# Mixture-of-experts tiles: tokens turned by VectorE in 32x32 blocks instead of by TensorE

## Chip, cores, metric

The kernel runs on 1 core of one Trainium2 chip. The metric is the device time of one execution in microseconds (us). Before the change it is 1062.39 us, the median of 3 runs (1062.15 to 1063.95).

## What is computed

The reference is an attention layer whose output feeds a mixture of experts. The attention has 8 batches, 8 heads, 576 positions and head size 64, and a bias that a small network makes of relative positions. Its output, 4608 tokens of 512 numbers, goes to 8 experts, one expert per token:

```
logits = x @ w_gate + modality_bias[modality_id]
e_idx = argmax(logits)
...
h = maximum(x[mask] @ w1[e], 0.0)
out[mask] = gate_w[mask, None] * (h @ w2[e])
```

`w1[e]` is 512 x 1024 and `w2[e]` 1024 x 512, all in float32.

## The kernel before

The attention part and the routing take the first 600 us or so. Routing (`route_steps`) writes each token's row, its 512 numbers, its gate and its index, into a table `xg` in device memory (516 columns), sorted by expert. The rest of the time goes to the experts.

**Tiles.** Each expert's rows are worked in tiles of 256 tokens (`tile`, L1201). The first five tiles (t = 0 to 4, `moe_first`, L1264) use experts that have a full tile before the last batch is routed; what is left of the routing runs beside tiles 0 to 3 as hooks (`beside`). The others run in `moe_rest` (L1282); a few very small remainders (`tiny_steps`, L1332) are put between the steps of three of them. The tables with the order of the tiles are computed on the chip.

**One tile.** Every float32 operand is split in a high part, rounded to TensorE's fp32r format, and a low part, the rest; a product is three products of parts. For a tile:

- `phase1` (L1152): four steps `f2`, each with two groups of 12 matmuls of 256 columns. A group takes the 4 products (w1 high, x high), then the 4 of (w1 high, x low), then the 4 of (w1 low, x high). ScalarE then writes `hh`, the high part of relu (L1168), and VectorE `hl`, its low part (L1169).
- `phase2` (L1174): two halves, w = 0 and 1, of 128 tokens; each has 24 matmuls of 512 columns, first 16 that alternate `hh` and `hl` over the 8 chunks of w2 high, then 8 with w2 low. ScalarE scales the result by the gate into `mo` (L1191) and GpSimd writes it to the output rows with an indirect DMA (L1192).
- Beside phase 1, the second layer's weights are split in four parts (`wsplit(1, ...)`, L1128 on ScalarE, L1129 on VectorE); after it the first layer's weights for the next tile, in four parts (`wsplit(0, ...)`).
- After half w = 0 of phase 2, `middle` (L1229) calls `xprep(t + 1, w)` (L1139) for both halves of the next tile.

**xprep before.** `load_rows` (L1081) brings the tile's 256 rows as one DMA, 128 partitions by two neighbouring tokens of 516 columns, into `gx`. `xprep` turns one half: four TensorE transposes of 128x128 into a PSUM bank (L1146), a ScalarE copy from there to `xh` (L1149), and a VectorE subtraction that reads PSUM and `xh` and writes `xl` (L1150). GpSimd copies the gate and the index (L1143, L1144).

**First tile.** The preparation of tile 0 is a hook at the end of the attention: `xprep(0, 0)` and `xprep(0, 1)` in steps 0 and 1 after the last pair of heads (`first_tiles`, L1241).

**Queues.** All engines run their instructions in the order in which the program issues them (a manual schedule). SyncE issues the loads: `load_new(t + 2, 0)` after phase 2, the rows of tile t + 2 at the start of tile t (from t = 4 on), and w2 after phase 1. The weight loads carry a condition and move nothing when the expert stays the same. The first layer's weights come as one DMA of 2 MB into 128 partitions (L1076).

Of the kernel before, what the change touches and what calls it, by code (L numbers as in the profile page):

```python
# [11 lines left out]
F32 = mybir.dt.float32  # L12
# [4 lines left out]
ALU = mybir.AluOpType  # L17
# [4 lines left out]
P = 128  # L22
# [8 lines left out]
DM = H * D  # L31
F = 1024
NDC = DM // P
NFC = F // P
TS = 256
NS = 32
NT = 3
XW = DM + 4
# [24 lines left out]
def n_tiles(n_tok):  # L63


    return -(-(n_tok - E * NS) // TS), (n_tok + E * (TS - 1)) // TS
# [42 lines left out]
class Attn:  # L109
# [766 lines left out]
    def moe_early(self, cp):  # L876

        nc = self.nc
        lo, hi = n_tiles(self.n_tok)
        self.n_kt = self.n_tab // TS - 1  # L880
        self.T = hi
        self.sure = lo
        n_tt = max(E, hi + 1 - self.K)
        one = cp.tile([1, 2 * E + self.n_kt + n_tt], F32, name="one")
        nc.sync.dma_start(one, self.io["c_one"])
        self.eb, self.iota = one[:, 0:E], one[:, E : 2 * E]
        self.kt, self.tt = one[:, 2 * E : 2 * E + self.n_kt], one[:, 2 * E + self.n_kt :]
        self.gates = cp.tile([P, 4], F32, name="gates")
        self.gk = cp.tile([1, E, self.n_kt], F32, name="gk")
        self.ge = cp.tile([1, n_tt, E], F32, name="ge")  # L890
        self.tf = cp.tile([1, 4, n_tt], F32, name="tabf")
        self.ev = {nm: cp.tile([1, E], F32, name=nm) for nm in ("cnt", "off", "cum", "val", "taken", "start", "big", "lim")}
        self.pad = [cp.tile([1, 4 + E], F32, name=f"pad{k}") for k in range(3)]
        for t in self.pad:
            nc.vector.memset(t, 0.0)
        self.ev["nt"] = self.pad[0][:, 4:]
        self.ex = cp.tile([1, 1], F32, name="last_expert")
        nc.vector.memset(self.ex, -1.0)
        nc.vector.memset(self.ev["taken"], 0.0)
        self.tabs = {nm: cp.tile([1, 4, n], I32, name=f"tab_{nm}") for nm, n in (("first", max(1, self.K)), ("big", hi + 1 - self.K), ("tiny", E))}  # L900
        self.idt = cp.tile([P, 4], I32, name="idt")
        self.gl = cp.tile([1, n_tt, E], F32, name="gl")
        self.tl = cp.tile([1, n_tt], F32, name="tl")
        self.ids_q = [cp.tile([P, 1], I32, name=f"idsq{k}") for k in range(NT)]
        self.quad = cp.tile([P, 1], F32, name="quad")
        nc.sync.dma_start(self.quad, self.io["c_quad"])

        slots = self.NBm.rearrange("p (c q h) k -> p c q (h k)", c=4, q=NP)
        w = [slots[:, :, q, 0 : 2 * DM] for q in range(NP)]
        rest = [slots[:, :, q, 2 * DM : 2 * S] for q in range(NP)]  # L910
        self.wst, self.ws = [w[0], w[1]], [w[2], w[3]]
        self.xr = [slots[:, c, 2, XW * j : XW * j + XW] for c, j in ((0, 0), (1, 0), (3, 0), (0, 1), (1, 1))]
        self.lt = slots[:, 2, 2, 0:XW]
        self.hq = [rest[0], rest[3]]
        self.gx = [self.NBr[:, k : k + 2, 0:XW] for k in (0, 2)]
        d = self.n_pair % 2
        qt = [self.QK[k].rearrange("p a w -> p (a w)") for k in (d, 1 - d)]
        self.xh = [t[:, 0 : NDC * TS].rearrange("p (c w) -> p c w", c=NDC) for t in qt]
        self.xl = [t[:, NDC * TS : 2 * NDC * TS].rearrange("p (c w) -> p c w", c=NDC) for t in qt]

    def moe_tiles(self, st):
        tc = self.tc
        mp = st.enter_context(tc.tile_pool(name="mp", bufs=1))
        self.whi = [mp.tile([P, NDC, F], F32R, name="w1hi"), mp.tile([P, NFC, DM], F32R, name="w2hi")]
        self.wlo = [mp.tile([P, NDC, F], F32R, name="w1lo"), mp.tile([P, NFC, DM], F32R, name="w2lo")]
        self.hh = mp.tile([P, NFC, TS], F32R, name="hh")
        self.hl = mp.tile([P, NFC, TS], F32R, name="hl")
        self.mo = [mp.tile([P, DM], F32, name=f"mo{k}") for k in range(2)]
        pp = st.enter_context(tc.tile_pool(name="mps", bufs=1, space=PSUM))
        self.p1 = [pp.tile([P, 2, TS], F32, name=f"p1{k}") for k in range(3)]  # L930
        self.p2 = [pp.tile([P, DM], F32, name=f"p2{k}") for k in range(3)]
        self.at = {}
# [135 lines left out]
        return ("first", t) if t < self.K else ("big", t - self.K)  # L1068

    def load_w(self, nm, t, k, dst, cond=None):  # L1070
        e = self.reg(nm, t, 0, [mybir.EngineType.SP], E - 1)
        c = None if cond is None else self.reg(nm, t, cond, [mybir.EngineType.SP], 1)
        kw = {} if c is None else dict(cond=c)
        src = self.io[("moe_w1", "moe_w2")[k]][ds(e, 1), :, :].rearrange("o (c p) f -> p (o c) f", p=P)
        if k == 0:
            self.nc.sync.dma_start(dst, src, **kw)  # L1076
        else:
            for j in range(2):
                self.nc.sync.dma_start(dst[:, :, DM * j : DM * j + DM], src[:, j::2, :], **kw)

    def load_rows(self, t):  # L1081

        nm, k = self.place(t)
        off = self.reg(nm, k, 1, [mybir.EngineType.SP], E * self.n_tab - TS)
        self.nc.sync.dma_start(self.gx[t % 2], self.xg[ds(off, TS), :].rearrange("(p w) c -> p w c", w=2))

    def rows(self, t):
        return [self.gx[t % 2][:, w, :] for w in range(2)]

    def ids_of(self, t):  # L1090
        return [self.idt[:, (2 * t + w) % 4 : (2 * t + w) % 4 + 1] for w in range(2)]
# [44 lines left out]
        self.nc.scalar.copy(h, w)  # L1136
        self.nc.vector.tensor_tensor(l, w, h.bitcast(F32), op=ALU.subtract)

    def xprep(self, t, w):  # L1139
        nc = self.nc  # L1140
        ps = self.xbank().rearrange("p (c w) -> p c w", c=NDC)
        x = self.rows(t)[w]
        nc.gpsimd.tensor_copy(self.gate(t)[w], x[:, DM : DM + 1])  # L1143
        nc.gpsimd.tensor_copy(self.ids_of(t)[w], x[:, DM + 1 : DM + 2])  # L1144
        for c in range(NDC):
            nc.tensor.transpose(ps[:, c, :], x[:, P * c : P * c + P], self.idf)  # L1146
        sl = slice(P * w, P * w + P)
        xh, xl = self.xh[t % 2], self.xl[t % 2]
        nc.scalar.copy(xh[:, :, sl], ps)  # L1149
        nc.vector.tensor_tensor(xl[:, :, sl], ps, xh[:, :, sl].bitcast(F32), op=ALU.subtract)  # L1150

    def phase1(self, t, before, beside):  # L1152
        nc = self.nc
# [47 lines left out]
    def tile(self, t, beside=None, between=()):  # L1201

        parts = iter(range(NDC))
        beside = beside or (lambda: None)

        def split():
            self.wsplit(1, next(parts))
            beside()

        between = iter(between)  # L1210

        def ahead(f2):
            for f in itertools.islice(between, 1):
                f()
            if t:
                return
            for part in {0: (1,) if self.K else (0, 1), 1: (2,), 2: (3,)}.get(f2, ()):
                self.wsplit_cols(part)
            if f2 == 2:
                self.load_new(1, 0)  # L1220

        if t + 2 > self.K:
            self.moe_rows(t + 2)
        self.phase1(t, ahead, split)
        self.load_new(t + 1, 1)
        for c in range(NDC):
            self.wsplit(0, c)

        def middle(w):  # L1229
            if w == 0 and t + 1 < self.T:  # L1230
                for j in range(2):
                    self.xprep(t + 1, j)
            beside()

        self.phase2(t, middle)
        if t + 2 <= self.K:
            self.moe_rows(t + 2)
        if t + 2 <= self.T:
            self.load_new(t + 2, 0)

    def first_tiles(self):  # L1241

        nc = self.nc
        n = self.n_pair - NP
        at = {}

        def add(pair, u, f):
            at.setdefault((n + pair, u), []).append(f)

        for k, f in enumerate(self.first_table()):  # L1250
            add(*divmod(4 + k, 5), f)
        add(2, 3, lambda: self.load_w("first", 0, 0, self.wst[0]))
        add(2, 2, lambda: self.load_rows(0))
        add(3, 0, lambda: self.load_w("first", 0, 1, self.wst[1]))
        for w in range(2):
            add(4, w, lambda w=w: self.xprep(0, w))
        add(4, 3, lambda: self.wsplit_cols(0))
        return at

# [22 lines left out]
    def moe_rest(self, st):  # L1282
        tc, nc = self.tc, self.nc
# [6 lines left out]
        if K == 0:  # L1290
            self.moe_load(0)
            self.load_new(0, 1)
            for w in range(2):
                self.xprep(0, w)
            self.moe_load(1)
        first = self.sure - 2 * NT
        for t in range(K, self.sure):
            k, odd = divmod(t - first, 2)
# [146 lines left out]
```

## Time and profile before

| | |
|---|---|
| median of 3 runs | 1062.39 us |
| the profiled execution | 1062.4 us |
| its span, first to last instruction | 1060.5 us |
| granted TensorE clock, mean | 0.998 |
| TensorE matmul, busy | 1011.3 us (95%) |
| VectorE, busy | 742.7 us (70%) |
| ScalarE, busy | 666.9 us (63%) |
| GpSimd, busy | 304.4 us (29%) |
| SyncE DMA queue (q1), share of 16 DMA engines | 30.5% |

The page names engines PE (TensorE matmul), PEld (its weight loads), DVE (VectorE), ACT (ScalarE), POOL (GpSimd) and SP (SyncE). "L1146" is line 1146 of the kernel before. Busy time of matmuls overlaps, because they are pipelined: the distance from one start to the next is the time that one takes from the stream. An idle time in brackets stands ahead of a row's instruction, with the engine whose work ended it.

### The profile page before, as it was taken

The page shows a single profiled execution, that of the slowest core. Times are in us where ns is not written, and L with a number is a line of the kernel's source. Part 1 is how long each engine was busy: PE and PEld are TensorE (multiplying, and loading weights), DVE is VectorE, ACT ScalarE, POOL GpSimd, SP SyncE. Part 2 cuts the span into 40 slices and gives each one's busy share as a digit, 9 for nine tenths or more (in the row PEclk, how much of TensorE's full clock was granted, in tenths as well). Part 3 has the DMA queues.
Part 4 walks back from the last instruction along what each step waited for, and adds up shares of the span by engine and source line. Part 5 has one row for each costly group of instructions (what it writes and reads, how often), then busy time and mean ns, then how long its engine had stood idle before and what let it go on. Part 6 is the DMA issues. An engine that isn't in the chain of part 4 may idle for free. (4 is left out here: it accounts for less than half of the span.)

```text
span 1060.5 us, 22805 instructions
## 1 busy us (share of the span) xinstructions
PE 1011.3 (95%) x8388; PEld 801.6 (76%) x8388; DVE 742.7 (70%) x1566; ACT 666.9 (63%) x1284; POOL 304.4 (29%) x489
## 2 busy tenths in 40 slices
PE   6879999999999989999999999999999999999997
PEld 2357776767677767677676789999999999888896
DVE  7886678787787787877879676785556655554544
ACT  6777776777777767677676664455555545454544
POOL 1612333526335253352443411530010111111011
PEclk9999999999999999999999999999999999999999
DMA  6977723234242333343234410122113821152410
GB/s 151 191 158 141 190 54 71 62 66 102 47 78 69 69 76 69 58 93 65 58 74 131 137 41 30 61 86 70 41 41 133 297 67 46 65 184 73 166 42 24
DMA packets 225465, 97.52 MB, mean 92 GB/s; under 512 B 201262, under 2 KB 201646, under 8 KB 225346
## 3 DMA queue, kind: packets, MB, share of 16 engines
q1 hardware_dynamic: 219330, 76.96, 30.5%
q0 software_dynamic: 5920, 19.03, 5.0%
q8 instruction: 68, 1.11, 0.4%
q14 instruction: 51, 0.42, 0.1%
q10 hardware_dynamic: 96, 0.00, 0.0%
HBM read 134.94 MB, written 23.90 MB: 150 GB/s over the span
## 5 line engine op out<-in xcount | busy, mean ns | idle before, releaser
L431 ACT ACTIVATE Eb<-Eb,mn 128x576 f32<-128x576 f32 x288 | 221.7, 771 | 66.4 <-DVE mn L416 66.3
L416 DVE CUSTOM_DVE_ANT_0 Eb<-sps,NBm 128x576 f32<-128x576 f32 x256 | 183.6, 754 | 62.7 <-PE sps L402 53.8
L402 PE MATMUL sps<-QK 64*128 64x288 f32 (+1 forms) x1728 | 171.2, 309 | 2.3 <-DVE mn L416 2.0
L402 PEld LDWEIGHTS sps<-QK 64*128 64x128 f32 (+1 forms) x1728 | 133.8, 185 | 46.1 <-DVE mn L416 15.6
L1166 PE MATMUL p<-QK,w1hi 128*128 128x256 f32 x1136 | 160.9, 284 | 0.0
L446 PE MATMUL eps<-idf,Eb 128*128 128x128 f32 x1024 | 147.7, 279 | 10.6 <-DVE eT L333 8.2
L1169 DVE SCALAR_TENSOR_TENSOR hl<-p,hh 128x512 fp32r<-128x512 f32 x72 | 49.7, 691 | 148.5 <-ACT hh L1168 148.4
L1166 PEld LDWEIGHTS p<-QK,w1hi 128*128 128x128 f32 x1136 | 147.0, 192 | 2.9 <-issue 1.8
L500 PE MATMUL xps<-eT,vraw 128*64 128x288 f32 x1024 | 147.1, 412 | 0.0
L446 PEld LDWEIGHTS eps<-idf,Eb 128*128 128x128 f32 x1024 | 111.3, 140 | 41.4 <-issue 17.7
L1192 POOL DMA_INDIRECT out<-mo,idt x36 | 40.1, 1113 | 317.1 <-ACT QK L1149 234.1
L1168 ACT ACTIVATE hh<-p 128x512 fp32r<-128x512 f32 x72 | 43.1, 599 | 119.9 <-PE p L1166 113.8
L331 ACT ACTIVATE eT<-eps 128x512 f32<-128x512 f32 x160 | 95.0, 593 | 34.1 <-PE eps L446 25.5
L1183 PE MATMUL p<-w2hi,hh 128*128 128x512 f32 x288 | 114.2, 396 | 0.0
L1183 PE MATMUL p<-w2hi,hl 128*128 128x512 f32 x288 | 112.5, 391 | 0.0
L436 POOL COPY rem<-Eb 128x128 f32<-128x128 f32 x128 | 37.5, 294 | 248.2 <-ACT Eb L431 245.2
L500 PEld LDWEIGHTS xps<-eT,vraw 128*64 128x64 f32 x1024 | 65.3, 137 | 53.5 <-issue 19.6
L1129 DVE TENSOR_TENSOR w2lo<-NBm,w2hi 128x1024 fp32r<-128x1024 f32 x72 | 88.2, 1225 | 16.2 <-ACT w2hi L1128 16.2
L333 DVE COPY eT<-eps 128x512 f32<-128x512 f32 x128 | 87.1, 681 | 11.8 <-PE eps L446 11.5
L1166 PE MATMUL p<-QK,w1lo 128*128 128x256 f32 x568 | 91.3, 283 | 0.0
L1129 DVE TENSOR_TENSOR w1lo<-NBm,w1hi 128x1024 fp32r<-128x1024 f32 x72 | 83.2, 1220 | 0.0
L1191 ACT ACTIVATE mo<-p,gates 128x512 f32<-128x512 f32 x36 | 24.8, 690 | 89.4 <-PE p L1183 75.2
(211 smaller groups left out, 1646.2 us busy)
## 6 DMA issues: line engine op xcount, KB each, us to landing
NBm<-moe_w SPq DMA_DIRECT2D x23, 2048.0 KB
NBm<-moe_w SPq DMA_DIRECT2D x44, 1024.0 KB
NBr<-xg SPq DMA_DIRECT2D x20, 516.0 KB
kraw<-k SPq DMA_DIRECT2D x128, 72.0 KB
NBm<-xTb SPq DMA_DIRECT2D x32, 288.0 KB
vraw<-v SPq DMA_DIRECT2D x64, 128.0 KB
xg<-blank SPq DMA_DIRECT2D x9, 516.0 KB
qraw<-q SPq DMA_DIRECT2D x64, 72.0 KB
```

Source lines behind the costliest of these rows:

```text
L331: self.nc.scalar.activation(out, ps, AF.Copy, scale=scale)
L333: self.nc.vector.tensor_copy(out, ps)
L402: nc.tensor.matmul(self.sps[h][:, half, 0:HS], QK[o, q, qs], QK[o, k, HS * half : HS * half + HS], start=i == 0, stop=i == 2, skip_group_c ...
L416: nc.vector.tensor_tensor_reduce(out=e.rearrange("p (t w) -> p t w", t=2), in0=self.sps[h][:, :, 0:HS], in1=nb.rearrange("p (t w) -> p t w ...
L431: self.nc.scalar.activation(e, e, AF.Exp, bias=mn, scale=-1.0, accum_out=sm)
L446: nc.tensor.transpose(ps[:, k, :], e[:, part, P * k : P * k + P], self.idf)
L500: nc.tensor.matmul(ps[o, :], v[:, h, k, :], self.eT[:, h, k, sl], start=half == 1 and k == 0, stop=half == 0 and k == 3, tile_position=(0, ...
L1129: self.nc.vector.tensor_tensor(l, w, h.bitcast(F32), op=ALU.subtract)
L1166: nc.tensor.matmul(ps[:, a, :], w[:, c, fs], x[:, c, :], start=i == 0, stop=i == len(ops) - 1)
L1168: nc.scalar.activation(hh[:, sl, :], ps, AF.Relu)
L1169: nc.vector.scalar_tensor_tensor(hl[:, sl, :], ps, 0.0, hh[:, sl, :].bitcast(F32), op0=ALU.max, op1=ALU.subtract)
L1183: nc.tensor.matmul(ps, h[:, f, sl], m[:, f, :], start=i == 0, stop=i == len(ops) - 1)
```

## The change

The tile's tokens are turned on VectorE. `load_rows` issues five DMAs: for each of four column blocks of 128, the 256 rows of that block land in 32 partitions, token 32a + r in partition r of the block, its 128 numbers at place a; a fifth DMA brings gate and index. One VectorE transpose of 128x1024 in 32x32 blocks (new L1163) then gives a tile `xt` with the hidden dimension on partitions, in the order 32 rows of each 128 per chunk. The rows of w1 are loaded in the same order, by four DMAs into 32 partitions each. The eight TensorE transposes go, and so does the PSUM bank that they used; the ScalarE copy and the VectorE subtraction become one instruction each, of 128x1024, with both inputs in SBUF. The load for the tiny remainders and all of w2 stay as they were.

```diff
     def load_w(self, nm, t, k, dst, cond=None):
...
+        if k == 0 and nm != "tiny":
+            for g in range(NDC):
+                rows = src[:, P * g : P * g + P, :].rearrange("o (c p) f -> p (o c) f", p=32)
+                self.nc.sync.dma_start(dst[32 * g : 32 * g + 32, :, :], rows, **kw)
+            return
...
     def load_rows(self, t):
...
-        self.nc.sync.dma_start(self.gx[t % 2], self.xg[ds(off, TS), :].rearrange("(p w) c -> p w c", w=2))
+        gx, rows = self.gx[t % 2], self.xg[ds(off, TS), :]
+        for g in range(NDC):
+            self.nc.sync.dma_start(
+                gx[32 * g : 32 * g + 32, 0 : NDC * TS].rearrange("r (a x) -> r a x", x=P),
+                rows[:, P * g : P * g + P].rearrange("(a r) x -> r a x", r=32),
+            )
+        self.nc.sync.dma_start(
+            gx[:, NDC * TS : NDC * TS + 4].rearrange("p (w x) -> p w x", w=2),
+            rows[:, DM : DM + 2].rearrange("(w p) x -> p w x", p=P),
+        )
...
-    def xprep(self, t, w):
-        nc = self.nc
-        ps = self.xbank().rearrange("p (c w) -> p c w", c=NDC)
-        x = self.rows(t)[w]
...
-        for c in range(NDC):
-            nc.tensor.transpose(ps[:, c, :], x[:, P * c : P * c + P], self.idf)
-        sl = slice(P * w, P * w + P)
+    def xprep(self, t, x):
...
         xh, xl = self.xh[t % 2], self.xl[t % 2]
-        nc.scalar.copy(xh[:, :, sl], ps)
-        nc.vector.tensor_tensor(xl[:, :, sl], ps, xh[:, :, sl].bitcast(F32), op=ALU.subtract)
+        x = x.rearrange("p (c w) -> p c w", c=NDC)
+        nc.vector.transpose(x, gx[:, 0 : NDC * TS].rearrange("p (a c i) -> p c a i", c=NDC, i=32))
+        nc.scalar.copy(xh, x)
+        nc.vector.tensor_tensor(xl, x, xh.bitcast(F32), op=ALU.subtract)
...
             if w == 0 and t + 1 < self.T:
-                for j in range(2):
-                    self.xprep(t + 1, j)
+                self.xprep(t + 1, self.xt)
...
-        for w in range(2):
-            add(4, w, lambda w=w: self.xprep(0, w))
+        add(4, 0, lambda: self.xprep(0, self.Eb[:, next(self.e_next)].rearrange("p h s -> p (h s)")[:, 0 : NDC * TS]))
```

Where instructions move, in the order of one engine. First TensorE in the middle of phase 2 of an ordinary tile (`p_...` is a PSUM tile of the result, `xps` the bank of the transposes, `NBr` the memory of `gx`), before and then after:

```order
L1183 MATMUL p_7581<-w2hi,hl 128x512
L1183 MATMUL p_7581<-w2lo,hh 128x512 x8
L1146 MATMUL xps_77<-idf,NBr 128x128 x4
L1146 MATMUL xps_78<-idf,NBr 128x128 x4
L1183 MATMUL p_7582<-w2hi,hh 128x512
```

```order
L1198 MATMUL p_7580<-w2hi,hl 128x512
L1198 MATMUL p_7580<-w2lo,hh 128x512 x8
L1198 MATMUL p_7581<-w2hi,hh 128x512
L1198 MATMUL p_7581<-w2hi,hl 128x512
L1198 MATMUL p_7581<-w2hi,hh 128x512
```

Half w = 1 now follows half w = 0 with nothing between them.

Then VectorE at the same place (`QK` is the memory of `xh` and `xl`), before and after:

```order
L1129 TENSOR_TENSOR w2lo<-NBm,w2hi 128x1024
L1129 TENSOR_TENSOR w1lo<-NBm,w1hi 128x1024 x4
L1150 TENSOR_TENSOR QK_73<-xps_77,QK_73 128x4x128
L1150 TENSOR_TENSOR QK_73<-xps_78,QK_73 128x4x128
L1169 SCALAR_TENSOR_TENSOR hl<-p_7579,hh 128x512
```

```order
L1143 TENSOR_TENSOR w2lo<-NBm,w2hi 128x1024
L1143 TENSOR_TENSOR w1lo<-NBm,w1hi 128x1024 x4
L1163 STREAM_TRANSPOSE xt<-NBr 128x1024
L1165 TENSOR_TENSOR QK_73<-xt,QK_73 128x1024
L1184 SCALAR_TENSOR_TENSOR hl<-p_7578,hh 128x512
```

The two subtractions are now a transpose and one subtraction, and between those two ScalarE's copy must run.

Last ScalarE at the end of the attention, where tile 0 is prepared (`eT` and `rT` are the turned attention weights), before and after:

```order
L331 ACTIVATE eT<-eps_717 128x4x128
L1149 CAST QK_72<-xps_78 128x4x128
L331 ACTIVATE eT<-eps_716 128x4x128
L331 ACTIVATE rT<-xps_77 128x512
L1149 CAST QK_72<-xps_78 128x4x128
L331 ACTIVATE xTb_95<-xps_77 128x288
```

```order
L331 ACTIVATE eT<-eps_717 128x4x128
L1164 CAST QK_72<-Eb 128x1024
L331 ACTIVATE eT<-eps_716 128x4x128
L331 ACTIVATE rT<-xps_78 128x512
L331 ACTIVATE xTb_95<-xps_77 128x288
```

The whole copy of tile 0 now stands ahead of the `eT` and `rT` copies, where only its first half stood.

## Rows read from the trace of the kernel before

**Rows 1.** The page, part 1: busy us, share and instructions of each engine.
```profile
PE 1011.3 (95%) x8388; PEld 801.6 (76%) x8388; DVE 742.7 (70%) x1566; ACT 666.9 (63%) x1284; POOL 304.4 (29%) x489
```

**Rows 2.** Waits of PE, 640 to 1060 us: total us, times, longest; the whole answer.
```profile
PE p L1365 <- DVE ht L1358: 0.6, 3, 0.2
```

**Rows 3.** Timeline of PE, an ordinary tile: start us, us, engine, line, what.
```profile
827.87 1.12 PE L1166 MATMUL p<-QK,w1hi 128*128 128x256 f32 x8
828.83 0.64 PE L1166 MATMUL p<-QK,w1lo 128*128 128x256 f32 x4
...
839.38 0.40 PE L1183 MATMUL p<-w2hi,hh 128*128 128x512 f32 x1
...
844.86 1.04 PE L1146 MATMUL xps<-idf,NBr 128*128 128x128 f32 x8
...
851.22 1.11 PE L1166 MATMUL p<-QK,w1hi 128*128 128x256 f32 x8
```

**Rows 4.** Groups of instructions by line: count, busy us, mean ns, idle before.
```profile
L1146 PE MATMUL xps<-idf,NBr 128*128 128x128 f32 x152 | 19.9, 273 | 0.2 <-DVE QK L1150 0.2
L378 DVE STREAM_TRANSPOSE qT<-qraw 128x640 f32<-128x640 f32 x32 | 26.8, 836 | 0.0
L378 DVE STREAM_TRANSPOSE kT<-kraw 128x576 f32<-128x576 f32 x32 | 24.8, 774 | 0.0
L1128 ACT CAST w1hi<-NBm 128x1024 fp32r<-128x1024 f32 x72 | 70.4, 1055 | 0.0
L1129 DVE TENSOR_TENSOR w1lo<-NBm,w1hi 128x1024 fp32r<-128x1024 f32 x72 | 83.2, 1220 | 0.0
```

**Rows 5.** Timeline of DVE, ACT and POOL in the same tile.
```profile
842.30 4.62 DVE L1129 TENSOR_TENSOR w1lo<-NBm,w1hi 128x1024 fp32r<-128x1024 f32 x4
845.78 1.06 ACT L1149 CAST QK<-xps 128x512 fp32r<-128x512 f32 x2
846.66 1.12 POOL L1192 DMA_INDIRECT out<-mo,idt  x1 [16.00 <-ACT QK L1149]
846.84 1.28 DVE L1150 TENSOR_TENSOR QK<-xps,QK 128x512 fp32r<-128x512 f32 x2
```

**Rows 6.** Timeline of tile 0: phase 2 begins, and the subtractions for tile 1.
```profile
627.00 0.47 PE L1183 MATMUL p<-w2hi,hh 128*128 128x512 f32 x1
635.36 1.29 DVE L1150 TENSOR_TENSOR QK<-xps,QK 128x512 fp32r<-128x512 f32 x2
```

**Rows 7.** Timeline from the end of tile 2 to the end of tile 3.
```profile
683.68 1.27 DVE L1150 TENSOR_TENSOR QK<-xps,QK 128x512 fp32r<-128x512 f32 x2
688.00 2.01 DVE L956 TENSOR_TENSOR pad<-pad 1x8 f32<-1x8 f32 x2
688.93 1.05 POOL L845 TENSOR_TENSOR NBm<-NBm,rec 64x512 f32<-64x512 f32 x1
699.40 0.40 PE L1183 MATMUL p<-w2hi,hh 128*128 128x512 f32 x1
700.59 0.67 DVE L1169 SCALAR_TENSOR_TENSOR hl<-p,hh 128x512 fp32r<-128x512 f32 x1
707.86 1.27 DVE L1150 TENSOR_TENSOR QK<-xps,QK 128x512 fp32r<-128x512 f32 x2
```

**Rows 8.** Timeline at the end of the attention, where tile 0 is prepared.
```profile
605.87 0.69 DVE L1150 TENSOR_TENSOR QK<-xps,QK 128x512 fp32r<-128x512 f32 x1 [0.63 <-ACT QK L1149]
606.21 0.62 ACT L331 ACTIVATE rT<-xps 128x512 f32<-128x512 f32 x1
607.64 0.71 PE L491 MATMUL xps<-rT,vrem 128*64 128x288 f32 x4
```

**Rows 9.** SP's timeline (two rows), and one window: us, five engines, PEclk, DMA, GB/s.
```profile
800.29 0.39 SPq L1076 DMA_DIRECT2D NBm<-moe_w  x1
848.36 0.56 SPq L1085 DMA_DIRECT2D NBr<-xg  x1
```
```profile
812.00:814.00 2.00, 2.00 (x19) 2.00 (x18) 1.23 (x1) 0.65 (x3) 0.00 (x0) 1.00 0.00 0
```

More of the change, by code (lines that the diff above doesn't have):

```diff
@@ L914, in moe_early @@
         self.hq = [rest[0], rest[3]]
-        self.gx = [self.NBr[:, k : k + 2, 0:XW] for k in (0, 2)]
+        self.gx = [self.NBr[:, k : k + 2, :].rearrange("p a s -> p (a s)") for k in (0, 2)]
         d = self.n_pair % 2
@@ L927, in moe_tiles @@
         self.hl = mp.tile([P, NFC, TS], F32R, name="hl")
+        self.xt = mp.tile([P, NDC * TS], F32, name="xt")
         self.mo = [mp.tile([P, DM], F32, name=f"mo{k}") for k in range(2)]
@@ L1073, in load_w @@
         kw = {} if c is None else dict(cond=c)
-        src = self.io[("moe_w1", "moe_w2")[k]][ds(e, 1), :, :].rearrange("o (c p) f -> p (o c) f", p=P)
+        src = self.io[("moe_w1", "moe_w2")[k]][ds(e, 1), :, :]
+        if k == 0 and nm != "tiny":
[3 more added lines that the diff above has]
+            return
+        src = src.rearrange("o (c p) f -> p (o c) f", p=P)
         if k == 0:
@@ L1084, in load_rows @@
         off = self.reg(nm, k, 1, [mybir.EngineType.SP], E * self.n_tab - TS)
-        self.nc.sync.dma_start(self.gx[t % 2], self.xg[ds(off, TS), :].rearrange("(p w) c -> p w c", w=2))
-    def rows(self, t):
-        return [self.gx[t % 2][:, w, :] for w in range(2)]
+        gx, rows = self.gx[t % 2], self.xg[ds(off, TS), :]
[8 more added lines that the diff above has]
+        )
     def ids_of(self, t):
@@ L1137, in wsplit_cols @@
         self.nc.vector.tensor_tensor(l, w, h.bitcast(F32), op=ALU.subtract)
-    def xprep(self, t, w):
+    def xprep(self, t, x):
         nc = self.nc
-        ps = self.xbank().rearrange("p (c w) -> p c w", c=NDC)
-        x = self.rows(t)[w]
-        nc.gpsimd.tensor_copy(self.gate(t)[w], x[:, DM : DM + 1])
-        nc.gpsimd.tensor_copy(self.ids_of(t)[w], x[:, DM + 1 : DM + 2])
-        for c in range(NDC):
-            nc.tensor.transpose(ps[:, c, :], x[:, P * c : P * c + P], self.idf)
-        sl = slice(P * w, P * w + P)
+        gx = self.gx[t % 2]
+        for w in range(2):
+            at = NDC * TS + 2 * w
+            nc.gpsimd.tensor_copy(self.gate(t)[w], gx[:, at : at + 1])
+            nc.gpsimd.tensor_copy(self.ids_of(t)[w], gx[:, at + 1 : at + 2])
         xh, xl = self.xh[t % 2], self.xl[t % 2]
-        nc.scalar.copy(xh[:, :, sl], ps)
-        nc.vector.tensor_tensor(xl[:, :, sl], ps, xh[:, :, sl].bitcast(F32), op=ALU.subtract)
+        x = x.rearrange("p (c w) -> p c w", c=NDC)
+        nc.vector.transpose(x, gx[:, 0 : NDC * TS].rearrange("p (a c i) -> p c a i", c=NDC, i=32))
+        nc.scalar.copy(xh, x)
+        nc.vector.tensor_tensor(xl, x, xh.bitcast(F32), op=ALU.subtract)
     def phase1(self, t, before, beside):
@@ L1292, in moe_rest @@
             self.load_new(0, 1)
-            for w in range(2):
-                self.xprep(0, w)
+            self.xprep(0, self.xt)
             self.moe_load(1)
```

## The prediction

> **What bounds the kernel now.** I read the page's busy shares first, then TensorE's waits, then the timeline of one tile, then the rows of the engines that would take over the work. PE is busy 95% of the span [rows 1]; that alone does not say that it is the bound, since matmuls overlap. The list of its waits does: from 640 to 1060 us PE waited 0.6 us in all [rows 2]. In the expert tiles every instruction taken from PE's stream therefore shortens the time, until another engine is late. VectorE has room on the average (70%), but what counts is whether it is ready at the hand-over from one tile to the next.
>
> One ordinary tile lasts 851.22 - 827.87 = 23.35 us [rows 3]. Half w = 0 of phase 2 takes 844.86 - 839.38 = 5.48 us, and the transposes plus half w = 1 take 851.22 - 844.86 = 6.36 us. The eight transposes so cost 0.88 us of the stream, not the 8 x 273 ns that their busy time [rows 4] suggests. Matmuls of phase 1 follow each other at (828.83 - 827.87) / 8 = 0.12 us, those of phase 2 at 5.48 / 24 = 0.228 us.
>
> **What the change removes.** 152 transposes [rows 4] are 19 preparations of eight: one at the end of the attention, 18 in tiles. In tiles: 18 x 0.88 = **15.8 us** off PE's path. The sums below go against the profiled execution, 1062.4 us (span 1060.5), which is the median of the runs within 0.1 us.
>
> **What it adds, on the new chain.** Per tile VectorE turns 128x1024. Rows of the same operation give 774 ns for 576 columns and 836 for 640 [rows 4], 0.97 ns a column; 384 more make 836 + 372 = 1208 ns, and up to 1236 at 1.04 ns, taken as 1.22 us. But those rows read each partition straight through, and the new one hops between runs of 32 numbers; no row shows that. The lower bound is 1.2 us, the upper one twice, 2.4 us; I take 1.22, since the nearest row is the same operation with the same blocks. Then ScalarE's copy of 128x1024, 1.055 us, and VectorE's subtraction, 1.22 us, both from rows of equal shape [rows 4]. The chain is 1.22 + 1.05 + 1.22 = 3.5 us and serial: VectorE waits for ScalarE in the middle. Before, ScalarE's copies (845.78) ran beside VectorE's weight splits (842.30 to 846.92), and the subtractions took 1.28 us [rows 5].
>
> *Ordinary tile.* VectorE is free for it at 846.84 [rows 5], so `xl` would be ready at 850.34. PE would reach the next tile at 851.22 - 0.88 = 850.34; its first four matmuls need only `xh` (ready at 849.1), the fifth needs `xl`, at 850.34 + 4 x 0.12 = 850.82. Margin: 0.48 us, less the hand-offs between engines. It was some 3.6 us. I forecast no stall in the 13 ordinary hand-overs (after tiles 4 to 16), but the cover is thin.
>
> *Tile 0.* The chain starts at 635.36 and ends at 638.86. PE needs `xl` at 627.00 + 2 x 5.48 + 0.48 = 638.44 [rows 6]: **+0.4 us**. Tiles 1 and 2 I take as covered, like the ordinary ones.
>
> *Tile 3.* Here VectorE works off the table of the remaining tiles without a pause. The chain of tile 2 starts at 683.68 and takes 3.5 us where 1.27 were, so what follows starts 2.2 us later. Part of it comes back: the two small subtractions and additions of L956 took 2.01 us because GpSimd was at L845 until 689.98 [rows 7], and that wait now falls on a queue that is behind anyway; I estimate a lag of 0.8 us (between 0 and 2). Then the last `hl` ends at 700.59 + 0.67 + 0.8 = 702.06, while PE, 0.88 earlier, wants it 13 matmuls into phase 2, at 698.52 + 13 x 0.228 = 701.48: 0.6 us. `xl` ends at 707.86 + 0.8 + 3.5 = 712.16, wanted at 698.52 + 0.6 + 10.96 + 0.48 = 710.56: 1.6 us. Together **+2.2 us** (1.4 without a lag, 3.4 with 2 us).
>
> *End of the attention.* VectorE is free at 605.87 - 0.63 = 605.24 [rows 8]. The transpose ends at 606.46, ScalarE's whole copy at 607.51, and only then come `eT` and `rT` of 0.6 us each, done at 608.7. The matmuls of L491 wait for `rT` and started at 607.64: **+1.0 us**. PE's own eight transposes less give nothing there, as it waits. Bounds: -0.8 (PE's saving counts after all) to +1.5.
>
> *Loads.* The row load is one issue of 0.56 us on SP [rows 9]; five make about 2.8 us. Those at 848.36 are for a preparation one tile later, at 846.84 + 23.35 = 870.2, so this is hidden by some 19 us. Real w1 loads are rare: the condition lets data move only where the expert changes, which in the expert tiles I find once, at the issue at 800.29. That load with the row load behind it had ended by 812, as the window from there on moved nothing [rows 9]; ScalarE splits these weights one tile period before the rows at 842.30, less one copy: at 817.9. It is hidden by about 6 us, and I cost it at nothing. GpSimd's copies of gate and index keep number and size.
>
> Sum: -15.8 + 1.0 + 0.4 + 2.2 = **-12.2 us**, 1050.2 us.
>
> [...] The subtraction that read PSUM and SBUF now reads SBUF twice. The rows show what that can cost: L956, SBUF only, stood while GpSimd ran L845 [rows 7]. [...]
>
> **The rivals.**
> - *The turn is slow (the slower side).* If hopping between blocks doubles the transpose to 2.44 us, the chain is 4.7 us and each ordinary hand-over stalls 1.22 - 0.48 = 0.74 us or, with hand-offs, up to 0.9: 13 x 0.85 = 11 us. Tiles 0 to 3 and the attention add about 1.2 each, tile 3 twice: 7 us. -12.2 + 18 = +6, **1068 us**. The point of decision is a transpose of about 2.1 us. For it: the margin of 0.48 and the unseen access pattern. Against: the operation works in 32x32 blocks in the rows too. Chance 0.11, with less slow forms.
> - *GpSimd meets `xl`.* A scatter of 1.12 us on `xl` exceeds the margin by 0.64: 13 x 0.7 = 9 us, **1059 us**. Against: it would have to start 2 us later than now. Chance 0.05.
> - *The w1 load is late.* Four DMAs that each reach a quarter of the partitions may move at half the rate: the 11.7 us from the issue (800.29) to the quiet window (812) [rows 9], which hold the row load too, become at worst 23.4 and end at 823.7, 5.8 us past 817.9. Half of that, less the margin, would stall PE once by some 2.5 us: **1053 us**. [...] Chance 0.12.
> - *Everything is covered.* If tile 3 and the attention lose nothing, 1062.4 - 15.8 - 0.8 = **1045.8 us**. Chance 0.12.
>
> The forecast has 0.60.
>
> **The numbers.** A measurement can tell 0.2% (2.1 us) here. Forecast, late load and full cover are faster: 0.84, and most of the GpSimd case, 0.86 in all. Slower by more than that is the slow turn at its worse half and beyond, 0.09; 0.05 lies between. The range runs from full cover, 1045.5, to 1058, which leaves out the slow turn and the GpSimd case, 0.16.
>
> **What would show it.** Right: no L1146 rows, phase 2 of an ordinary tile 10.96 us, tile period 22.47, transposes near 1.22 us, ScalarE's copy 1.05, PE's wait list short except for VectorE's `xl` after tile 0 and `hl` and `xl` in tile 3, L491 near 608.6. Wrong: a PE wait for `xl` in every tile, a transpose above 1.6 us, a subtraction stretched beside GpSimd, or ScalarE waiting for a weight DMA near 817.

## The result, and the profile after

The changed kernel takes **1052.47 us** (median of 4 runs, 1051.08 to 1053.35); the kernel before, on the same chip, 1063.17 us (4 runs, 1062.15 to 1064.0). The ratio is 0.9901, with a 95% interval from 0.9887 to 0.9915: 10.7 us faster, where 12.2 were forecast. The profiled execution took 1052.45 us, its span is 1050.7 us, and the mean granted clock of TensorE 0.995.

The page, part 1, of the changed kernel, answering to [rows 1] (busy us, share, instructions):

```profile
PE 997.9 (95%) x8236; PEld 786.4 (75%) x8236; DVE 764.5 (73%) x1566; ACT 666.8 (63%) x1265; POOL 304.7 (29%) x489
```

The 152 transposes are gone from PE, and DVE is busy 21.8 us longer. The rest is a question of place. I cut the span at three instructions that both kernels have: VectorE's last turn in the attention (L378), the first matmuls of tile 0's phase 1, and the last eight matmuls of the last tile's phase 2. First the timeline of the kernel before, these three rows (start us, us, engine, line, what):

```profile
580.01 0.77 DVE L378 STREAM_TRANSPOSE kT<-kraw 128x576 f32<-128x576 f32 x1
...
614.50 3.12 PE L1166 MATMUL p<-QK,QK 128*128 128x256 f32 x24
...
1051.13 1.98 PE L1183 MATMUL p<-w2lo,hh 128*128 128x512 f32 x8
```

The same three in the changed kernel:

```profile
580.83 0.77 DVE L378 STREAM_TRANSPOSE kT<-kraw 128x576 f32<-128x576 f32 x1
...
617.81 3.14 PE L1181 MATMUL p<-QK,QK 128*128 128x256 f32 x24
...
1041.12 1.98 PE L1198 MATMUL p<-w2lo,hh 128*128 128x512 f32 x8
```

| stretch | before, us | after, us | difference | forecast |
|---|---|---|---|---|
| start to the last turn | 580.01 | 580.83 | +0.82 | 0 (same program) |
| last turn to tile 0 | 34.49 | 36.98 | **+2.49** | +1.0 |
| tile 0 to the last matmuls | 436.63 | 423.31 | **-13.32** | -13.2 |
| to the end of the span | 9.37 | 9.58 | +0.21 | 0 |
| span | 1060.5 | 1050.7 | -9.8 | -12.2 |

So the expert tiles gave what was forecast, and the missing part lies at the end of the attention. The first row is scatter: over the ten profiles of this study the same early program took between 578.37 and 580.83 us.

**Ordinary tile.** The timeline of the changed kernel, all engines, the hand-over to a tile that answers to [rows 3, 5]:

```profile
826.09 1.11 PE L1181 MATMUL p<-QK,w1hi 128*128 128x256 f32 x8
...
837.60 0.40 PE L1198 MATMUL p<-w2hi,hh 128*128 128x512 f32 x1
...
844.86 1.12 POOL L1207 DMA_INDIRECT out<-mo,idt  x1 [16.00 <-ACT mo L1206]
845.05 1.24 DVE L1163 STREAM_TRANSPOSE xt<-NBr 128x1024 f32<-128x1024 f32 x1
...
846.32 1.05 ACT L1164 CAST QK<-xt 128x1024 fp32r<-128x1024 f32 x1 [2.23 <-DVE xt L1163]
...
847.40 1.23 DVE L1165 TENSOR_TENSOR QK<-xt,QK 128x1024 fp32r<-128x1024 f32 x1 [1.12 <-ACT QK L1164]
848.51 1.11 PE L1181 MATMUL p<-QK,w1hi 128*128 128x256 f32 x8
```

The period is 848.51 - 826.09 = 22.42 us (before 23.35). The new chain is there: turn, copy, subtraction, each waiting for the one before, and VectorE idle for 1.12 us in the middle. It ends at 847.40 + 1.23 = 848.63; PE wants `xl` four matmuls into phase 1, at 848.51 + 0.48 = 848.99. The margin is 0.36 us, and PE does not stop. The scatter on GpSimd is over at 845.98, before `xl` starts.

The groups by line of the changed kernel: what VectorE's two new operations cost.

```profile
L1163 DVE STREAM_TRANSPOSE xt<-NBr 128x1024 f32<-128x1024 f32 x18 | 22.3, 1240 | 0.0
L1165 DVE TENSOR_TENSOR QK<-xt,QK 128x1024 fp32r<-128x1024 f32 x18 | 22.1, 1226 | 20.1 <-ACT QK L1164 20.1
```

The turn that hops between blocks takes 1240 ns, just above the 1208 to 1236 that the straight rows of 576 and 640 columns gave [rows 4].

**Tiles 0 and 3.** PE's waits in the changed kernel, 640 to 1050 us (total us, times, longest), without the one row of [rows 2], which is still there with the same 0.6 us:

```profile
PE p L1181 <- DVE QK L1165: 0.9, 2, 0.5
PE p L1181 <- ACT QK L1164: 0.8, 1, 0.8
PE p L1198 <- DVE hl L1184: 0.3, 1, 0.3
```

All three are new, and the timeline of the changed kernel shows where they are: one after tile 0, the others in tile 3 and after it (compare [rows 6, 7]).

```profile
642.32 0.74 PE L1181 MATMUL p<-QK,w1hi 128*128 128x256 f32 x4 [0.37 <-DVE QK L1165]
...
704.08 0.50 PE L1198 MATMUL p<-w2hi,hl 128*128 128x512 f32 x1 [0.30 <-DVE hl L1184]
...
713.11 0.74 PE L1181 MATMUL p<-QK,w1hi 128*128 128x256 f32 x4 [0.80 <-ACT QK L1164]
...
714.37 0.74 PE L1181 MATMUL p<-QK,w1hi 128*128 128x256 f32 x4 [0.52 <-DVE QK L1165]
```

**End of the attention.** The timeline of the changed kernel, answering to [rows 8]:

```profile
607.27 1.04 ACT L1164 CAST QK<-Eb 128x1024 fp32r<-128x1024 f32 x1 [1.12 <-DVE Eb L1163]
...
608.22 0.59 ACT L331 ACTIVATE eT<-eps 128x512 f32<-128x512 f32 x1
...
608.71 0.59 ACT L331 ACTIVATE rT<-xps 128x512 f32<-128x512 f32 x1
608.87 0.66 PE L452 MATMUL eps<-idf,Eb 128*128 128x128 f32 x4 [2.00 <-ACT eT L331]
609.45 0.80 PE L491 MATMUL xps<-rT,vrem 128*64 128x288 f32 x4
610.03 2.14 PE L500 MATMUL xps<-eT,vraw 128*64 128x288 f32 x8
```

The copy of tile 0 stands ahead of `eT` and `rT` on ScalarE as forecast, PE stands for 2.00 us, and L491 comes at 609.45 (before 607.64; 0.82 of the difference were there at the last turn, so the stop itself is worth +1.0). What was not forecast is the last row: eight matmuls of L500 take 2.14 us. The timeline of the kernel before has them at 1.14:

```profile
608.18 1.14 PE L500 MATMUL xps<-eT,vraw 128*64 128x288 f32 x8
```

Two windows of the changed kernel (us, the five engines, PEclk, DMA, GB/s) say why:

```profile
610.00:612.00 2.00, 2.00 (x12) 1.02 (x10) 0.77 (x2) 0.00 (x0) 0.00 (x0) 0.50 0.09 21
612.00:614.00 2.00, 2.00 (x18) 1.22 (x16) 0.22 (x1) 0.06 (x1) 0.00 (x0) 0.66 0.00 0
```

After the stop the granted clock is 0.50 in the first of them and 0.66 in the second. Before, no window from 560 to 640 us was below 1.00.

**Loads.** The windows of the changed kernel over the one real w1 load, issued at 800.32:

```profile
804.00:806.00 2.00, 2.00 (x19) 2.00 (x18) 0.00 (x0) 0.69 (x1) 0.00 (x0) 1.00 1.07 348
...
808.00:810.00 2.00, 2.00 (x19) 2.00 (x18) 1.35 (x2) 0.66 (x2) 0.14 (x1) 1.00 0.99 201
810.00:812.00 2.00, 2.00 (x19) 2.00 (x18) 1.45 (x2) 1.21 (x2) 0.00 (x0) 1.00 1.05 200
...
814.00:816.00 2.00, 2.00 (x16) 1.87 (x15) 1.23 (x1) 0.71 (x3) 0.00 (x0) 1.00 0.23 58
```

It moves 200 to 201 GB/s in the windows from 808 to 812, more ahead of them (348 in one window), and the last data, with the rows behind it, move early in the window from 814 (58 of some 200 GB/s), until about 814.6. ScalarE splits these weights from 816.81 on, without a wait. The margin is 2.2 us, where 6 were forecast.

### The profile page after: what moved, and what is told of

The parts are those of the page before. It is cut to its first block, busy times and chain, and to the rows that moved or that the text cites. A ratio compares the mean times of both kernels' runs of the same rounds, so it can differ in the third digit from the quotient of the medians.

```text
span 1050.7 us, 22872 instructions
## 1 busy us (share of the span) xinstructions
PE 997.9 (95%) x8236; PEld 786.4 (75%) x8236; DVE 764.5 (73%) x1566; ACT 666.8 (63%) x1265; POOL 304.7 (29%) x489
## 5 line engine op out<-in xcount | busy, mean ns | idle before, releaser
L500 PE MATMUL xps<-eT,vraw 128*64 128x288 f32 x1024 | 148.7, 416 | 0.0
L500 PEld LDWEIGHTS xps<-eT,vraw 128*64 128x64 f32 x1024 | 65.9, 138 | 54.1 <-issue 20.5
L1181 PEld LDWEIGHTS p<-QK,w1lo 128*128 128x128 f32 x568 | 78.3, 192 | 0.0
```

Source lines behind the costliest of these rows:

```text
L500: nc.tensor.matmul(ps[o, :], v[:, h, k, :], self.eT[:, h, k, sl], start=half == 1 and k == 0, stop=half == 0 and k == 3, tile_position=(0, ...
L1181: nc.tensor.matmul(ps[:, a, :], w[:, c, fs], x[:, c, :], start=i == 0, stop=i == len(ops) - 1)
```

## The experiments

Theory: the gain is PE's stream time; what the change loses, it loses where the serial chain turn, copy, subtraction is longer than the cover: at the end of the attention, after tile 0 and around tile 3. Rivals: the gain comes from elsewhere; the loss at the attention is the stop alone, or the stop and the clock; the loads cost something. The first four runs share one set of runs of the kernel before (median 1062.04 us, 11 runs), the last four another (1064.18 us, 9 runs). Between the sets I compare ratios; where a place decides, the stretches of the table above, read from the same three rows of each profile.

| version | time, us | ratio (95%) | last turn to tile 0 | expert tiles |
|---|---|---|---|---|
| before | | 1 | 34.49 | 436.63 |
| the change | 1052.47 | 0.9901 (0.9887 to 0.9915) | 36.98 | 423.31 |
| the change, again | 1051.88 | 0.9893 (0.9878 to 0.9909) | 36.99 | 423.35 |
| copy of tile 0 later | 1047.45 | 0.9859 (0.9843 to 0.9876) | 33.14 | 423.34 |
| stop filled | 1049.59 | 0.9889 (0.9871 to 0.9908) | 35.31 | 423.24 |
| dead transposes | 1065.27 | 1.0025 (1.001 to 1.0041) | 35.31 | 437.27 |
| turn twice | 1072.13 | 1.0097 (1.008 to 1.0114) | 38.23 | 442.63 |
| turn early | 1048.14 | 0.9848 (0.9833 to 0.9862) | 37.66 | 420.86 |
| both | **1046.2** | **0.9834** (0.9821 to 0.9848) | 33.14 | 421.03 |
| w1 in one load | 1050.82 | 0.988 (0.9865 to 0.9895) | 36.94 | 423.47 |

**1. Eight dead transposes back in each tile.** They write a PSUM bank that nobody reads, at the place where the eight stood.

```diff
             if w == 0 and t + 1 < self.T:
+                for _ in range(2):
+                    ps = self.xbank().rearrange("p (c w) -> p c w", c=NDC)
+                    for c in range(NDC):
+                        self.nc.tensor.transpose(ps[:, c, :], self.gx[(t + 1) % 2][:, P * c : P * c + P], self.idf)
                 self.xprep(t + 1, self.xt)
```

> The change as it is, with the eight TensorE transposes per tile put back as work that nobody reads, in the middle of phase 2, where they were. Theory (the gain is TensorE's own time in the stream, 0.93 us per tile in 18 tiles): tile period back from 22.42 to 23.35 us, 18 x 0.93 = 16.7 us lost, of which about 1.5 us come back because tiles 0 and 3 no longer wait for xl as long; 1067 us. Rival (the gain comes from the PSUM bank and the engines' waits around the transposes): at most half of it is lost, 1053 to 1060 us.

Measured: 1065.27 us. The timeline of PE in this version, one tile:

```profile
852.38 1.11 PE L1181 MATMUL p<-QK,w1hi 128*128 128x256 f32 x8
...
869.37 1.03 PE L1249 MATMUL xps<-idf,NBr 128*128 128x128 f32 x8
...
875.70 1.12 PE L1181 MATMUL p<-QK,w1hi 128*128 128x256 f32 x8
```

The period is 23.32 us again, that of before, and the expert tiles take 437.27 us: 13.96 more than in the change, which had won 13.32, so the rival falls. Expected were 16.7 - 1.5 = 15.2; more of the stalls came back, since of PE's waits for `xl` only one of 0.4 us is left. In an ordinary tile all of the gain is PE's stream time; VectorE's new work is covered there.

**2. The turn done twice.** The second one overwrites the first with the same numbers.

```diff
-        nc.vector.transpose(x, gx[:, 0 : NDC * TS].rearrange("p (a c i) -> p c a i", c=NDC, i=32))
+        for _ in range(2):
+            nc.vector.transpose(x, gx[:, 0 : NDC * TS].rearrange("p (a c i) -> p c a i", c=NDC, i=32))
```

> The change with VectorE's turn done twice, so that the chain to xl is 1.24 us longer. Theory (the ordinary hand-over has a margin of 0.36 us, and beyond it TensorE waits): each of the 13 ordinary hand-overs waits 0.9 us, 11.5 us; tiles 0 to 2 and the end of the attention 1.2 us each, tile 3 about 2.5 us; sum 18 us, 1070 us, slower than before the change. Rival (the margin is larger, since TensorE can run ahead on xh or the split weights can come later): under 6 us, 1053 to 1058 us.

Measured: 1072.13 us. PE's waits in this version, 640 to 1050 us:

```profile
PE p L1182 <- DVE QK L1166: 8.1, 17, 0.5
PE p L1182 <- ACT QK L1165: 3.3, 4, 2.1
...
```

Now `xl` is late at every one of the 17 hand-overs, and the ordinary period is 883.22 - 859.72 = 23.50 us: of 1.24 us more work 1.08 reach the end, where 0.9 were expected. The cover took up 0.16 us of the delay and not the 0.36 of the margin; what took the rest was not followed up. The expert tiles take 19.3 us more than in the change and the end of the attention 1.25, where 18 were expected in all, and the time is 2 us above the 1070 stated. The rival of a larger margin falls. This is the forecast's rival of the slow turn, and it shows how thin the cover is.

**3. Tile 0's copy and subtraction two steps later.** The turn stays in step 0; the ScalarE copy moves behind `eT` and `rT`.

```diff
-        add(4, 0, lambda: self.xprep(0, self.Eb[:, next(self.e_next)].rearrange("p h s -> p (h s)")[:, 0 : NDC * TS]))
+        x0 = []
+
+        def turn0():
+            x0.append(self.Eb[:, next(self.e_next)].rearrange("p h s -> p (h s)")[:, 0 : NDC * TS])
+            self.xprep(0, x0[0], parts=False)
+
+        add(4, 0, turn0)
+        add(4, 2, lambda: self.xparts(0, x0[0]))
```

> Tile 0's ScalarE copy and VectorE subtraction are moved two steps later, behind the eT and rT copies; its turn stays where it is. Theory (TensorE stood 2.0 us for eT and rT because the whole copy of tile 0 ran first, and its granted clock then fell to 0.50 for 3 us or so): the wait of L452 goes below 0.5 us, the clock stays at 1.00 from 606 to 616 us, and the start of tile 0's phase 1 is 2.5 to 3.3 us earlier than after the change; 1049.5 us where the change gives 1052.5. Rival (the fall of the clock has another cause, such as the matmuls that follow): only the wait goes, 1.0 us, and the clock still falls; 1051.5 us.

Measured: 1047.45 us. The timeline of this version at the same place:

```profile
605.29 0.60 ACT L331 ACTIVATE rT<-xps 128x512 f32<-128x512 f32 x1
...
606.04 1.05 ACT L1172 CAST QK<-Eb 128x1024 fp32r<-128x1024 f32 x1
606.05 0.71 PE L491 MATMUL xps<-rT,vrem 128*64 128x288 f32 x4
606.58 1.14 PE L500 MATMUL xps<-eT,vraw 128*64 128x288 f32 x8
```

The stop is gone, the eight matmuls of L500 take 1.14 us again, and the clock is 1.00 in every window from 604 to 618. From the last turn to tile 0 it is 33.14 us: 3.84 less than in the change, more than the 2.5 to 3.3 expected (and 1047.45 us where 1049.5 were), and 1.35 less than before. PE's own eight transposes count once it no longer waits: in the trace before they hold 0.44 us of the stream (from 604.19) and 0.49 (from 606.62), and 0.23 of waiting ahead of the second four goes with them. The last 0.19 lie behind L491, in every changed version whose clock stays at 1.00 there.

**4. The stop filled.** The order of the change stays, ScalarE's too; 16 dead transposes keep PE busy while it waits.

```diff
+        def fill():
+            for _ in range(4):
+                for c in range(NDC):
+                    nc.tensor.transpose(self.sps[0][:, 0, P * c : P * c + P], self.gx[0][:, P * c : P * c + P], self.idf)
+
+        add(4, 1, fill)
```

> The change as it is, with 16 transposes of data that nobody reads put into TensorE's stream ahead of L452, where it stood for 2.0 us. They take 16 x 0.11 = 1.8 us. Theory (the stop itself costs 1.0 us, the lower clock after it another 1.5 us): L491 starts where it did after the change, give or take 0.3 us, but the clock stays at 1.00, so that phase 1 of tile 0 starts 1.5 us earlier; 1051.0 us where the change gives 1052.5. Rival (the clock falls whatever TensorE does there, or the transposes lie on the path): 1052.5 to 1054 us.

Measured: 1049.59 us. The timeline of PE in this version:

```profile
604.24 1.91 PE L1274 MATMUL sps<-idf,NBr 128*128 128x128 f32 x16
606.42 0.66 PE L452 MATMUL eps<-idf,Eb 128*128 128x128 f32 x4 [0.27 <-ACT eT L331]
...
607.54 1.14 PE L500 MATMUL xps<-eT,vraw 128*64 128x288 f32 x8
```

`eT` comes no earlier: L491 starts 28.64 us after the last turn, in the change 28.62, as expected. But the clock stays at 1.00 from 604 to 618, and the stretch takes 35.31 us: 1.67 less than in the change, where 1.5 were expected. By the times alone nothing is decided (the intervals of the ratios overlap). The stretch shows what the full clock is worth; that the fill is what held the clock is not shown by this one profile, since a version with the stop unfilled kept it too (see 5).

**5. The change once more.** No edit.

> The change itself once more, for the TensorE clock after the stop at the end of the attention. If the fall to half clock belongs to this order of instructions, this profile shows 0.50 again at 609 to 613 us and phase 1 of tile 0 starts at about 617; if it depends on more than the order of instructions, as a version with the same stop that kept full clock suggests, the clock may stay at 1.00 and phase 1 then starts 1.5 us earlier. Time 1050.5 to 1053.5 in either case.

Measured: 1051.88 us, in the range expected, and 36.99 us from the last turn to tile 0, the same as in the first profile of the change to 0.01 us. A window of this run:

```profile
608.00:610.00 2.00, 2.00 (x10) 0.98 (x8) 0.85 (x2) 0.00 (x0) 0.06 (x1) 0.50 0.23 52
```

Six profiles have this stop of 2.0 us or more (the change twice, versions 1, 2, 6 and 8 here); in five of them the clock falls right after it, to between 0.50 and 0.55 in the lowest window of 2 us. In the dead-transposes version it does not. The timeline of PE there:

```profile
607.74 0.66 PE L452 MATMUL eps<-idf,Eb 128*128 128x128 f32 x4 [2.01 <-ACT eT L331]
...
608.87 1.14 PE L500 MATMUL xps<-eT,vraw 128*64 128x288 f32 x8
```

PE stands for 2.01 us, the windows read 1.00, and the stretch is 35.31 us. So the stop alone is worth 35.31 - 34.49 = +0.82 us, and the clock 36.98 - 35.31 = +1.67. In the four profiles without the stop (before, versions 3, 4 and 7) it never falls there.

Why one stop of six kept full clock is open. Its length does not decide: near 63 us, in a part that the change leaves as it was, PE stops for 2.06 to 3.00 us in all ten profiles of this study. In five of them the clock falls right after it, to between 0.50 and 0.57 in the lowest window of 2 us; in the other five it stays at 1.00. In the kernel before, with a stop of 3.00 us, it stayed; in the changed kernel, with 2.93 us, it fell. The window behind the stop, first before, then after:

```profile
64.00:66.00 2.00, 2.00 (x32) 1.14 (x24) 1.99 (x6) 0.93 (x3) 0.00 (x0) 1.00 0.89 214
```

```profile
64.00:66.00 2.00, 2.00 (x20) 0.74 (x16) 1.04 (x4) 0.00 (x0) 0.00 (x0) 0.50 0.95 203
```

**6. The turn of the next tile ahead of the weight splits.** ScalarE's copy can then run beside VectorE's splits; only the subtraction stays at the hand-over.

```diff
+        if t + 1 < self.T:
+            self.xprep(t + 1, self.xt, parts=False)
         for c in range(NDC):
             self.wsplit(0, c)
...
             if w == 0 and t + 1 < self.T:
-                self.xprep(t + 1, self.xt)
+                self.xparts(t + 1, self.xt)
```

> The turn of the next tile is issued before the weight splits of the tile, so that ScalarE's copy no longer stands between a turn and a subtraction that follow each other on VectorE. Margin theory (the chain turn, copy, subtraction is serial at the hand-over, and where VectorE is behind it stalls TensorE): the chain at the hand-over falls from 3.5 to 1.2 us plus a copy that runs beside, the stall after tile 0 goes and tile 3's shrinks from 2.4 to about 1, ordinary tiles stay at 22.4 us; the end of the attention is as in the change. Time 1050 to 1051.5, 1 to 2.5 us under the change. Rival (the stalls of tiles 0 and 3 come from VectorE's total work there, not from the order of the chain): 1052.5, as the change, with the same two waits for xl.

Measured: 1048.14 us. The timeline of this version, an ordinary hand-over:

```profile
838.64 1.24 DVE L1167 STREAM_TRANSPOSE xt<-NBr 128x1024 f32<-128x1024 f32 x1
...
842.12 1.04 ACT L1172 CAST QK<-xt 128x1024 fp32r<-128x1024 f32 x1
...
844.31 1.22 DVE L1173 TENSOR_TENSOR QK<-xt,QK 128x1024 fp32r<-128x1024 f32 x1
...
846.63 1.11 PE L1189 MATMUL p<-QK,w1hi 128*128 128x256 f32 x8
```

`xl` is ready at 845.53, 1.58 us ahead of its use at 847.11, where the margin was 0.36; the period stays 22.4 us, since it had no stall. The waits of PE from 640 to 1050 us shrink to 0.3 us for `xl`, now after tile 2, where the four weight splits ahead of the subtraction took 6.45 us instead of 4.6; and the expert tiles take 2.49 us less than in the repeat of the change: 0.6 in tile 1, 1.0 in tile 3, 0.9 in tile 4. That is the upper end of what the order of the chain was expected to give, and the rival falls. The median is 3.7 us lower than the repeat's and below the range expected; the other 1.2 us are not explained by this profile, which is that of the longest of the five runs, with a mean granted clock of 0.991 where the other four had 0.993 to 0.996.

**7. Both.** Edits 3 and 6 together.

> Tile 0's copy and subtraction two steps later, and the turn of each next tile early. Margin theory and the stop at the end of the attention are separate losses, so their gains add: the stop's 4.5 us (first run of that part alone) and 1 to 2 us of the early turn, 1045 to 1047. Rival (the early turn takes VectorE's time from the splits that phase 1 needs, and gives back what it wins): 1047.5 to 1049.

Measured: 1046.2 us, the fastest version, in the range expected. The stretches are 33.14 us, as in version 3, and 421.03 us, within 0.2 of version 6: the two gains add. The ratio of 0.9834 is 16 to 19 us under the kernel before by its interval.

**8. w1 in one load, in the old order of rows.**

```diff
-        if k == 0 and nm != "tiny":
+        if False:
```

> The first layer's weights are loaded by one DMA in their old row order; left out is the matching row order, so the product pairs hidden numbers with other rows of w1. It prices the four-way load. Theory (the four-way load is slower by half but hidden, with some 2 us left): the load at 800 us moves at 370 to 420 GB/s again and ends about 3.5 us earlier, ScalarE waits for nothing either way, and the time is that of the change within 1 us, 1051.5 to 1053. [...]

Measured: 1050.82 us, between the range of the theory and that of the rival that the loads cost something (1048 to 1050.5), so the time alone decides nothing; the interval of its ratio overlaps that of the change. Its two stretches agree with the repeat's within 0.12 us: the four-way load of w1 costs nothing there. The rows still come in five loads in this version, so those are not priced. The windows over the load, issued at 798.48 in this run:

```profile
804.00:806.00 2.00, 2.00 (x19) 2.00 (x18) 0.41 (x1) 1.04 (x2) 0.00 (x0) 1.00 1.01 414
...
808.00:810.00 2.00, 2.00 (x19) 2.00 (x19) 1.29 (x2) 1.37 (x2) 0.60 (x1) 1.00 0.97 224
810.00:812.00 2.00, 2.00 (x19) 2.00 (x18) 1.28 (x2) 1.28 (x2) 0.00 (x0) 1.00 0.05 16
```

The weights move at up to 414 GB/s again, and the load with the rows behind it ends early in the window from 810 (16 of some 220 GB/s), about 11.7 us after the issue, where the four-way load needed 814.6 - 800.32 = 14.3: 2.6 us, where 3.5 were expected. The slow load is real, and hidden.

## Why the prediction came out as it did

- **TensorE is the bound, and its eight transposes are stream time: right.** Version 1 puts them back and gets the period of before. The size was 0.93 us a tile (23.35 - 22.42), not 0.88, so 18 x 0.93 = 16.7 us where 15.8 were forecast: phase 2 without the break takes 848.51 - 837.60 = 10.91 us, a little less than twice the 5.48 of its first half.
- **The chain of 3.5 us and the margin of 0.48 us: right.** The chain runs from 845.05 to 848.63, 3.58 us with its hand-offs, and the margin is 0.36. No ordinary tile stalls. The choice of 1.22 us for a turn that no row showed, from straight rows of the same operation, was right within 0.02.
- **Tile 0: right in its wait** (0.37 for 0.4).
- **Tile 3: right in place, somewhat small.** The waits are those forecast, first `hl`, then `xl`, and the copy. From the start of phase 1 of tile 0 to that of tile 5 it is 736.41 - 617.81 = 118.60 us, before 734.55 - 614.50 = 120.05: 1.45 less, where five ordinary savings would be 4.65. So the stalls of tiles 0 and 3 cost 3.2 us with the gaps in the stream that they leave, against 0.4 + 2.2 = 2.6. That and the larger saving nearly cancel, so that -13.32 came out for -13.2 is in part luck.
- **End of the attention: the step that was mis-sized.** The forecast had ScalarE's copy ahead of `eT` and `rT`, L491 later by 1.0 us, with an upper bound of +1.5. The delay is right; the term measured +2.49. It took the matmuls behind the wait at the rate that they have in the trace of before, and did not ask what a stop does to them. The dead-transposes version has the same stop and kept the clock, version 4 keeps the wait for ScalarE and fills the stop: both measure +0.82. So the other 1.67 us are the half clock after the stop: the eight matmuls of L500 took 1.0 us more, the 24 behind them 0.6 (3.67 against 3.08). The clock fell after this stop in five of six profiles (0.50 to 0.55 in the lowest window); why not in the sixth, no run shows.
- **PE's own eight transposes give nothing at that place: right for the change** and the reason why version 3 gains more than the stop: 1.35 us under before.
- **Loads at nothing: right, with less room than thought.** For a part of the load the rate was halved, as the rival had it (200 to 201 GB/s in the windows from 808 to 812, against up to 414 with w1 in one transfer into all 128 partitions, version 8), but from the issue to the last data it took 14.3 us, against 11.7 in version 8, and ended at 814.6, not at the worst case of 823.7. The forecast had 6 us of room; 2.2 are left. The five row issues, put at 2.8 us on SP, took 3.6 us from 849.41 on and 7.2 from 835.83 on; VectorE waited for no DMA from 640 to 1050 us.
- **GpSimd and the subtraction: right.** `xl` takes 1226 ns as an average of 18; nothing stretched it. What a scatter on `xl` would have cost, no run shows. Four weight subtractions took 4.61 us beside an indirect DMA of GpSimd (L849, 678.99 to 684.66 in the trace of before), as much as in an ordinary tile (4.62); beside GpSimd's product and copy (L845, L848, from 682.50 in version 6) they took 6.45.

What is left of the difference between forecast (1050.2) and measurement (1052.45 in the profiled execution, 2.25 us): the attention's end +1.5, the expert tiles -0.1, +0.8 of scatter before the changed part begins, +0.2 at the end of the span and -0.15 outside it.

## What to carry to other kernels

Moving work off the bounding engine gives back its stream time as long as no other engine comes late (0.93 us in an ordinary tile here), but look at the program's few irregular places (first tile, a tile beside other work) one by one: that is where a longer serial chain loses its cover. Where a chain crosses engines, issue its first link early, so that the second runs beside other work of the first engine; here that was worth 2.5 us, and putting a copy behind the ones that others wait for another 3.8. A stop of TensorE is priced with what the clock can do after it, not by its length alone (0.82 us for the stop here, 1.67 for the clock).

## What the runs showed of the hardware

- After a stop of TensorE of 2.0 to 3.3 us at the end of the attention the granted clock fell in five of six profiles, to between 0.50 and 0.55 in the lowest window of 2 us; it cost 1.67 us in the change, more than the stop (0.82). After the stop near 63 us it fell in five of ten profiles, and not by length: once after 2.06 us, and not after 3.00. In the version with the turn done twice, another fall (0.50 from 718 to 720) follows the longest wait after tile 3 (2.1 us). With the stop filled by 16 useless transposes it did not fall (1.00 in the windows from 604 to 618; one profile, so not shown to be the fill's doing).
- Runs of one kernel differ by some 4 us, and this goes with the clock: of the five runs of version 6 the one with mean granted clock 0.996 took 1046.55 us, those with 0.994 took 1046.97 and 1048.14, with 0.993 1050.14, and with 0.991 1050.59.
- Four DMAs in a row, each into another 32 partitions, moved 200 to 348 GB/s together with the loads of rows behind them (windows from 804 to 812 of the change), where one into all 128 partitions with the same loads behind it moved up to 414 (version 8). One of the four alone was not run.
- VectorE's 32x32 transpose of float32 with a source in runs of 32 numbers and jumps between them (1240 ns for 1024 columns) is just above what the straight ones give (836 for 640 and 774 for 576, so 1208 to 1236).
